# Attention and MoE in one kernel: ScalarE's exponentials ahead of the copies, weight pieces loaded four ahead, buffers moved

## The chip, the cores and the metric

The kernel runs on one core of a Trainium2 chip. The metric is device microseconds of one execution, the median of several runs. The engines are named as in the profile: PE is TensorE (PEld its weight loads), DVE is VectorE, ACT is ScalarE, POOL is GpSimd, SP is SyncE, whose queue issues nearly all DMAs.

## What is computed

Attention with rotary embedding over q, k, v of 4 x 8 heads x 576 x 64, then a feed-forward block with a convolution of three taps and a gate:

```python
q_rot, k_rot = (rotate(q), rotate(k))
scores = scale * np.matmul(q_rot, k_rot.transpose(0, 1, 3, 2))
scores = scores - np.max(scores, axis=-1, keepdims=True)
attn = np.exp(scores)
attn = attn / (np.sum(attn, axis=-1, keepdims=True) + 1e-09)
x = np.matmul(attn, v)              # heads side by side: 4 x 576 x 512
h = np.maximum(x @ w_in, 0.0)       # 512 x 1024
conv_out[:, t] = sum(conv_w[k] * hp[:, t + k] for k in range(3))
out = (h / (1.0 + np.exp(-conv_out))) @ w_out
```

All is in 32-bit floats. The weights arrive as 64-bit floats and are turned into 32-bit ones on the chip, each as a high and a low part.

## The kernel before

**Pairs and steps.** Two heads form a pair; there are 16 pairs, and each is worked in five steps (s = 0 to 4) of 128 rows of queries, the fifth with the last 64 rows of both heads. Steps are numbered through, n = 5p + s, from 0 to 79. For each step PE writes the scores into PSUM (`emit_S`, L254), DVE takes the negated row maxima of both heads (L269), ACT the exponentials of both with the row sums (L273). PE then transposes the result in 64 x 64 blocks (`emit_T`, L314, transposes L321) into two PSUM tiles, and ACT copies these two tiles to the buffer `pt` in SBUF (`out`, L337, copies through `evac`, L199). The next step's transposes go into the same two tiles. `emit_E` (L383, matmuls L389) multiplies the transposed probabilities of the pair before with v; in front of the MoE its result and that of `emit_Trem` (L352) lie in spare columns of the scores' PSUM tile, so the maxima of a step also wait for them. POOL applies the rotary embedding (L190, L193) to q and k of the coming pairs, DVE transposes them (L234, L237).

**Weights.** There are 16 pieces of 128 x 512 (`conv_w_piece`, L605): ACT takes the absolute value (L563), DVE does four passes (L566, L572, L577, L582), ACT writes the high part (L632), POOL the low one (L629). The first 13 pieces (`WEARLY`) are spread over steps 0 to 24, each load being issued by the last DVE pass of the piece three before; the buffer of a loaded piece exists four times. The last three pieces are placed by the table `LATEW`, which gives step and rank of their five parts.

**Order.** Each engine's order is the order in which the program emits. `at(n, rank, fn)` puts a function into step n; within a step the lower rank comes first. For steps below `WIDE` = 26 the ranks are: transposes 0, maxima 0.2, exponentials 0.3, parts of weight pieces 0.4, transposes of q and k 0.45, the next scores 0.5, `emit_E` 4, loads 18 to 19.6. From step 26 on, PSUM is laid out anew, with a pool for the MoE, and the MoE's units (`emit_M1`, L418, and `m2_half`, L527) are put between the steps. There, at step 26, the buffers of the MoE are opened and POOL clears their border columns (L783, L784); ACT's scaling by the first tap (L440) reads these borders.

**The lines of the change.** `emit_T` emitted the two copies directly after the transposes (L345); the last piece's first part stood in step 31 (L686); the load was issued three pieces ahead (L620); the MoE's buffers `rr` shared the pool `gpool` with the large buffer `gm` (L777 to L781).

Of the kernel before, what the change touches and what calls it, by code (L numbers as in the profile page):

```python
# [7 lines left out]
F32 = mybir.dt.float32  # L8
# [12 lines left out]
def attention_moe_kernel(ctx, tc, q, k, v, w_in, conv_w, w_out, tab, tabx, out):  # L21
# [9 lines left out]
    XW = HS + 2  # L31
# [43 lines left out]
    late = {"tail": False, "u": 0}  # L75
# [13 lines left out]
    def t_tile():  # L89
        return psum["t"].tile([128, 512], F32, tag="t", name="tp")  # L90
# [223 lines left out]
    def emit_T(p, s, h=None):  # L314
        if not h:
            tps[p] = [t_tile() for _ in range(2)]
        ps = tps[p]

        def turn(k, x, r):
            i = slice(64 * r, 64 * r + 64)  # L320
            nc.tensor.transpose(ps[r][:, 64 * k:64 * k + 64], x[i], idf[i, i])  # L321

        if s == 4:
            st = strem[p % 2]
            for t in range(4):
                for r in range(2):
                    turn(t, st[:, 128 * t:128 * t + 128], r)
            for r in range(2):
                turn(4, st[:, 512 - 64 * r:640 - 64 * r], r)
            evac("A", pt[:, 0:9:2, 512:S], ps[0][:, 0:320].rearrange("p (k c) -> p k c", k=5))  # L330
            evac("A", pt[:, 1:8:2, 512:S], ps[1][:, 0:256].rearrange("p (k c) -> p k c", k=4))
            evac("A", pt[64:128, 8, 512:S], ps[1][64:128, 256:320])
        else:
            for t in range(4):
                for r in range(2):
                    turn(2 * t + h, ST[p, s][:, h, 64 * h + 128 * t:64 * h + 128 * t + 128], r)
            def out():  # L337
                for r in range(2):
                    c = 128 * s + 64 * r
                    evac("A", pt[:, 0:8, c:c + 64], ps[r].rearrange("p (k c) -> p k c", k=8))  # L340

            if h and "m" in psum:
                at(late["n"], 2.2 if UNITS.get(late["n"]) == 2 else 1.6, out)
            elif h:
                out()  # L345

    def emit_Trem(p, s):
        x = ST[p, s].rearrange("p h k -> p (h k)")[:, 512:640]
# [249 lines left out]
    def load_w(i):  # L598
        src, _, _, kk, c = WPIECES[i]
        pool, bufs = wpool(i)  # L600
        t = pool.tile([128, 512], I64, tag="w64", name="w64", bufs=bufs + 1)
        nc.sync.dma_start(out=t, in_=src[kk * 128:kk * 128 + 128, c:c + 512])
        stage[i] = t

    def conv_w_piece(i):  # L605
        _, dh, dl, kk, c = WPIECES[i]
        box = {}

        def first():
            box["s"] = to_f32(*wpool(i), stage.pop(i), 512)  # L610
            box["s"][0]()

        def part(k):
            return lambda: box["s"][k]()

        def last():
            pool, bufs = wpool(i)
            box["w"] = pool.tile([128, 512], F32, tag="wf", name="wf", bufs=bufs)
            box["s"][4](box["w"])
            if i + 3 < WEARLY:  # L620
                load_w(i + 3)
            elif WEARLY <= i < len(WPIECES) - 2:
                load_w(i + 2)
            hi, lo = dh[:, kk, c:c + 512], dl[:, kk, c:c + 512]

            def low():
                for o in range(0, 512, 128):
                    w = slice(o, o + 128)
                    nc.gpsimd.tensor_tensor(out=lo[:, w], in0=box["w"][:, w], in1=hi[:, w].bitcast(F32), op=ALU.subtract)  # L629

            def high():
                nc.scalar.activation(out=hi, in_=box["w"], func=AF.Copy)  # L632

            if i < WEARLY:
                defer(2, lambda: (high(), low()))
            else:
                at(late["n"] + 1, 0.12, lambda: (high(), low()))

        return [first, part(1), part(2), part(3), last]

    def load_cw():
        t = stage["cw"] = ws.tile([32, 128], I64, tag="cw64", name="cw64", bufs=1)
        nc.gpsimd.memset(t.bitcast(I32), 0)
        nc.sync.dma_start(out=t[0:24, :], in_=conv_w.rearrange("k (c p) -> (k c) p", p=128))
# [26 lines left out]
    WEARLY = len(wcv) - 3  # L671
    COST = (1, 1, 0, 0, 1)
    wsteps = [(1, wcv[0][0])]
    for i in range(WEARLY):
# [8 lines left out]
    LATEW = (  # L683
# [3 lines left out]
    )  # L687
    plan = {}
    onpe = (0, 0.2, 0.5, 1, 2, 2.4, 3, 4, 10)
# [2 lines left out]
    def at(n, rank, fn):  # L692
        plan.setdefault(n, []).append((rank, len(plan.get(n, [])), fn))

    def emit():
        with tc.manual_schedule(engines=engines):
# [14 lines left out]
            load_v(0)  # L711
            load_w(2)
            load_cw()
            for p in range(1, NP):
                n = STEPS * p
                early = n - 10 >= WIDE - 1
                for i, part in enumerate("qk"):
                    if p > 1:
                        at(max(n - 10, WIDE) if early else n - 9 + 2 * i, 19.6 if early else 19, lambda p=p, part=part: load(p, part))
                    at(n - 8 + i if early else max(n - 6 + i, 0) if p > 1 else 0, 18, lambda p=p, part=part: rope(p, part))  # L720
                    at(n - 5 + i * (n - 10 < WIDE) if early else max(n - 4 + 2 * i, 2), 0.45, lambda p=p, part=part: emit_TQ(p, part))
                at(n + 1, 19, lambda p=p: load_v(p))
            for p in range(NP):
                n = STEPS * p
# [36 lines left out]
            for n, k in UNITS.items():  # L761
                for i in range(k):
                    blk, f = divmod(late["u"], NF)
# [5 lines left out]
            n = -1  # L769
            while any(plan.values()):  # L770
                n += 1
                late["n"] = n
                if n == WIDE:
                    wctx.close()
                    ectx.close()
                    psum_pools(actx, s=2, t=2, m=2)
                    gpool = ctx.enter_context(tc.tile_pool(name="gpool", bufs=1))  # L777
                    late["pc"] = ctx.enter_context(tc.tile_pool(name="pc", bufs=4))
                    late["po"] = ctx.enter_context(tc.tile_pool(name="po", bufs=1))
                    late["g"] = [gpool.tile([128, 2, NF, RA], F32R, name="gm")]  # L780
                    late["rr"] = [gpool.tile([128, XW + 1], F32, name=f"rr{i}") for i in range(4)]  # L781
                    for t in late["rr"]:
                        nc.gpsimd.memset(t[:, 0:1], 0.0)  # L783
                        nc.gpsimd.memset(t[:, XW:XW + 1], 0.0)  # L784
                if n == WIDE + 12:
                    lctx.close()
                    late["g"].append(ctx.enter_context(tc.tile_pool(name="gb", bufs=1)).tile([128, 2, NF, RING - RA], F32R, name="gb"))
                while plan.get(n):
                    e = min(plan[n], key=lambda e: e[:2])
                    plan[n].remove(e)  # L790
                    e[2]()
                    if e[0] in onpe and e[0] != (0 if n >= WIDE else 0.2):
                        tick()
# [72 lines left out]
```

## Time and profile before

| what | value |
|---|---|
| median of 3 runs | 490.39 us (490.19 to 491.83) |
| the profiled execution | 493.55 us, its span 491.8 us |
| mean granted clock of TensorE | 0.975 |
| busy: PE, DVE, ACT, POOL | 457.9, 355.7, 332.5, 300.9 us |
| chain that ended last: PE, DVE, ACT, DMA | 71%, 12%, 5%, 4% of the span |

The span runs from the first to the last instruction of the profiled execution; the execution's own time lies 1.75 us above it. Times in the rows are microseconds from the span's start. The busy time of PE is an upper bound, since matmuls are pipelined and their ends are modelled. The granted clock is a share of 2.4 GHz; the lower level is 1.2 GHz, a share of 0.5.

### The profile page before, as it was taken

The numbers are of one execution on the slowest core, as the hardware profiler recorded it, in microseconds if no ns is written. First come the engines' busy times: TensorE is split into PE (matmuls) and PEld (weight loads), VectorE is DVE, ScalarE is ACT, GpSimd is POOL, SyncE is SP. The second block draws the span as 40 slices with busy tenths as digits, with TensorE's granted clock in tenths as the row PEclk, the third lists the DMA queues.
The fourth block names the chain that finished last, engine by engine and source line by source line (L and its number), as shares of the span: only waits on it lengthen the run. The fifth ranks groups of instructions, "written<-read, shape, count | busy, mean of one in ns | idle before, by whom it ended". The sixth has DMA issues, their size and how long they took to land.

```text
span 491.8 us, 12405 instructions
## 1 busy us (share of the span) xinstructions
PE 457.9 (93%) x4572; PEld 361.2 (73%) x4572; DVE 355.7 (72%) x636; ACT 332.5 (68%) x951; POOL 300.9 (61%) x495
## 2 busy tenths in 40 slices
PE   1869879797898999999999999999999999999997
PEld 1436546464676788887979787878797979899886
DVE  5589978958598987686868686877774756467921
ACT  2587968777697878686878686868596864145510
POOL 3599889888669958485766757584721313244510
PEclk9989988979899899999999999999999999999999
DMA  8983885965445234253625190707020200100011
GB/s 224 168 175 104 168 191 112 172 146 119 97 93 109 37 73 98 62 98 75 93 61 110 38 131 19 150 14 140 29 61 13 60 13 25 45 21 23 0 63 44
DMA packets 140559, 42.71 MB, mean 87 GB/s; under 512 B 132156, under 2 KB 135252, under 8 KB 140500
## 3 DMA queue, kind: packets, MB, share of 16 engines
q1 hardware_dynamic: 139156, 41.54, 39.9%
q8 instruction: 36, 0.59, 0.5%
q10 hardware_dynamic: 1344, 0.39, 0.4%
q14 instruction: 23, 0.19, 0.1%
HBM read 37.12 MB, written 4.79 MB: 85 GB/s over the span
## 4 chain that ended last, share of the span: by engine, by line
PE 71%; DVE 12%; ACT 5%; DMA 4%; SPq 4%; POOL 3%; issue 2%; DVEq 0%; POOLq 0%; ACTq 0%
PE pm L428 13%; PE sp L261 12%; PE pm L537 11%; PE mt L517 10%; PE pm L389 10%; PE mt L428 7%; PE tp L321 5%; DVE negm L269 4%; DMA rq<-q 2%; ACT st L273 2%; POOL rk L190 2%; DVE wt L577 1%; DMA rd<-rt 1%; PE sp L389 1%; DVE wt L572 1%
## 5 line engine op out<-in xcount | busy, mean ns | idle before, releaser
L269 DVE TENSOR_REDUCE negm<-sp 128x1 f32<-128x576 f32 x144 | 102.6, 749 | 45.6 <-PE sp L261 30.3
L273 ACT ACTIVATE st<-sp,negm 128x576 f32<-128x576 f32 x128 | 93.8, 742 | 27.6 <-DVE negm L269 26.7
L261 PE MATMUL sp<-kT,qT 64*128 64x288 f32 (+4 forms) x556 | 103.5, 476 | 5.2 <-DVE kT L237 2.4
L199 ACT ACTIVATE pt<-tp 128x512 f32<-128x512 f32 (+3 forms) x176 | 84.0, 529 | 5.3 <-PE tp L321 4.8
L446 DVE SCALAR_TENSOR_TENSOR c<-rr,cw,c 128x288 f32<-128x288 f32 x128 | 79.4, 620 | 4.4 <-ACT c L440 0.2
L464 POOL TENSOR_TENSOR gm<-c,gm 128x288 fp32r<-128x288 f32 (+4 forms) x72 | 45.4, 635 | 52.7 <-ACT gm L463 52.5
L428 PE MATMUL pm<-xT,winh 128*128 128x290 f32 x352 | 75.9, 310 | 0.0
L190 POOL TENSOR_TENSOR rq<-rq,tabt 128x192 f32<-128x192 f32 x90 | 59.7, 696 | 14.5 <-DMA rq<-q 14.5
L261 PEld LDWEIGHTS sp<-kT,qT 64*128 64x128 f32 (+1 forms) x556 | 48.2, 182 | 26.3 <-issue 9.1
L410 POOL TENSOR_TENSOR xT<-xn,xT 128x290 fp32r<-128x290 f32 x32 | 28.1, 878 | 60.0 <-ACT xT L406 59.9
L321 PEld LDWEIGHTS tp<-idf,st 64*128 64x128 f32 x1024 | 43.2, 142 | 24.2 <-ACT st L273 13.2
L428 PEld LDWEIGHTS pm<-xT,winh 128*128 128x128 f32 x352 | 57.2, 192 | 1.8
L190 POOL TENSOR_TENSOR rk<-rk,tabt 128x192 f32<-128x192 f32 x90 | 54.9, 642 | 4.2 <-DVE c L455 4.2
L321 PE MATMUL tp<-idf,st 64*128 64x64 f32 x1024 | 48.6, 230 | 9.5 <-ACT st L273 9.4
L428 PE MATMUL pm<-xT,winl 128*128 128x290 f32 x176 | 52.6, 299 | 0.0
L389 PE MATMUL pm<-pt,vm 128*64 128x290 f32 x368 | 49.8, 411 | 0.4 <-ACT pt L199 0.4
L537 PE MATMUL pm<-wouth,gm 64*128 64x256 f32 x512 | 49.3, 282 | 0.0
L455 DVE SCALAR_TENSOR_TENSOR c<-c,rr 128x288 f32<-128x288 f32 x64 | 37.6, 609 | 9.6 <-ACT c L452 9.6
L537 PEld LDWEIGHTS pm<-wouth,gm 64*128 64x128 f32 x512 | 43.0, 185 | 0.0
L444 DVE TENSOR_SCALAR c<-rr,cw 128x288 f32<-128x288 f32 x56 | 24.0, 428 | 21.1 <-ACT rr L436 19.7
L537 PE MATMUL pm<-woutl,gm 64*128 64x256 f32 x256 | 38.8, 277 | 0.0
L389 PEld LDWEIGHTS pm<-pt,vm 128*64 128x64 f32 x368 | 25.6, 136 | 17.6 <-ACT pt L199 1.1
(119 smaller groups left out, 911.7 us busy)
## 6 DMA issues: line engine op xcount, KB each, us to landing
rq<-q SPq DMA_DIRECT2D x30, 144.0 KB
rq<-q SPq DMA_DIRECT2D x60, 72.0 KB
rk<-k SPq DMA_DIRECT2D x30, 144.0 KB
rk<-k SPq DMA_DIRECT2D x60, 72.0 KB
w<-moe_w_in SPq DMA_DIRECT2D x8, 512.0 KB
vm<-v SPq DMA_DIRECT2D x32, 128.0 KB
w<-moe_w_out SPq DMA_DIRECT2D x8, 512.0 KB
rb<-rd SPq DMA_DIRECT2D x16, 144.0 KB
```

Source lines behind the costliest of these rows:

```text
L190: nc.gpsimd.tensor_tensor(out=y, in0=y, in1=tabt[:, a:a + 3], op=ALU.mult)
L199: nc.scalar.activation(out=out, in_=in_, func=AF.Copy, scale=1.0 if sc is None else sc)
L261: nc.tensor.matmul(out=out, lhsT=qt[64 * h:64 * h + 64, c], rhs=kt[64 * h:64 * h + 64, a:a + n], start=True, stop=True)
L269: reds.setdefault((p, s), []).append(lambda: nc.vector.tensor_reduce(out=nm, in_=sc, axis=AX.XY if len(sc.shape) == 3 else AX.X, op=ALU.ma ...
L273: lambda: nc.scalar.activation(out=dst, in_=sc, func=AF.Exp, bias=nm, scale=1.0, accum_out=sm)
L321: nc.tensor.transpose(ps[r][:, 64 * k:64 * k + 64], x[i], idf[i, i])
L389: nc.tensor.matmul(out=xp[64 * h:64 * h + 64, :], lhsT=vmain[p][:, h, i, :] if i < 4 else vrem[p % 2][:, h, :], rhs=pt[:, 2 * i + h if i < ...
L428: nc.tensor.matmul(out=ps[:, 0:XW], lhsT=w[:, kk, fs], rhs=xT[:, xs, e, :], start=(i == 0), stop=(i == n - 1))
L446: nc.vector.scalar_tensor_tensor(out=c, in0=r[:, j + e:j + e + HS], scalar=cw[:, 8 * e + f:8 * e + f + 1], in1=c, op0=ALU.mult, op1=ALU.add,)
L464: nc.gpsimd.tensor_tensor(out=lo, in0=c[:, o:o + n], in1=hi.bitcast(F32), op=ALU.subtract)
L517: nc.tensor.matmul(out=ops[tt][:, 0:width], lhsT=g_tile(tt, f, e), rhs=w[:, f, cols], start=(f == 0 and i == 0), stop=(f == NF - 1 and i = ...
L537: nc.tensor.matmul(out=ps[r][:, 0:256], lhsT=g_tile(tt, f, e)[rows], rhs=w[rows, f, cols], start=(f == 0 and i == 0), stop=(f == NF - 1 an ...
```

## The change

It does four things. Below step 26 the two copies of a step's transposes are put at rank 0.32 of the step that emits the transposes, behind that step's exponentials (0.3). One more weight piece is loaded at the start, and each later load up to piece 12 is issued by the piece four before. The absolute value of the last piece moves from step 31 to step 32. The buffers `rr` get a pool of their own, opened first, and `gm` is opened last. The copies of the fifth step (s = 4) of a pair are emitted elsewhere (L330 to L332) and stay where they were.

```diff
             if h and "m" in psum:
                 at(late["n"], 2.2 if UNITS.get(late["n"]) == 2 else 1.6, out)
             elif h:
-                out()
+                at(late["n"], 0.32, out)
...
-            if i + 3 < WEARLY:
-                load_w(i + 3)
+            if i + 4 < WEARLY:
+                load_w(i + 4)
             elif WEARLY <= i < len(WPIECES) - 2:
                 load_w(i + 2)
...
-        ((31, 5.5), (33, 2.6), (33, 2.6), (34, 2.6), (34, 2.6)),
+        ((32, 5.5), (33, 2.6), (33, 2.6), (34, 2.6), (34, 2.6)),
...
             load_w(2)
             load_cw()
+            load_w(3)
...
                     psum_pools(actx, s=2, t=2, m=2)
-                    gpool = ctx.enter_context(tc.tile_pool(name="gpool", bufs=1))
+                    rpool = ctx.enter_context(tc.tile_pool(name="rpool", bufs=1))
+                    late["rr"] = [rpool.tile([128, XW + 1], F32, name=f"rr{i}") for i in range(4)]
                     late["pc"] = ctx.enter_context(tc.tile_pool(name="pc", bufs=4))
                     late["po"] = ctx.enter_context(tc.tile_pool(name="po", bufs=1))
+                    gpool = ctx.enter_context(tc.tile_pool(name="gpool", bufs=1))
                     late["g"] = [gpool.tile([128, 2, NF, RA], F32R, name="gm")]
-                    late["rr"] = [gpool.tile([128, XW + 1], F32, name=f"rr{i}") for i in range(4)]
```

ACT in step 16 (the fourth pair; step 16 emits the transposes of the probabilities of step 15), before; `pt<-tp` are the copies of the transposes, `st<-sp,negm` the exponentials, `wt` and `winh` parts of weight pieces:

```order
L632 ACTIVATE winh<-wf 128x512 [waits DVE_49]
L199 ACTIVATE pt<-tp 128x8x64 [waits PE_49] x2
L273 ACTIVATE st,sums<-sp,negm 128x576 [waits DVE_49]
L273 ACTIVATE st,sums<-sp,negm 128x576
L399 ACTIVATE xn<-sp 128x145 [waits Pool_49]
L563 ACTIVATE wt<-w_915 128x512 [waits DMAHW1_49]
```

and with the change:

```order
L632 ACTIVATE winh<-wf 128x512 [waits DVE_49]
L273 ACTIVATE st,sums<-sp,negm 128x576 [waits DVE_49,PE_49]
L273 ACTIVATE st,sums<-sp,negm 128x576
L199 ACTIVATE pt<-tp 128x8x64 [waits PE_49] x2
L399 ACTIVATE xn<-sp 128x145 [waits Pool_49]
L563 ACTIVATE wt<-w_796 128x512 [waits DMAHW7_49]
```

The two copies now stand behind both exponentials, and behind their wait for DVE's maxima. One wait holds for both exponentials.

SP's queue at the place that issued a load at 75.11 us, before (`rk` is k, `rd` the round trip of the row sums; `w_1023` is piece 10):

```order
L150 DMA rk<-k 32x18x32 [waits DMAHW6_49]
L151 DMA rk<-k 32x18x32 [waits DMAHW7_49]
L602 DMA w_1023<-moe_w_out 128x512 [waits DMAHW0_49,Activation_49]
L371 DMA rd<-rt 9x32 [waits DMAHW1_49,DVE_49]
L371 DMA rd<-rt 9x32 [waits DMAHW2_49]
```

and with the change (`w_1025` is piece 11):

```order
L150 DMA rk<-k 32x18x32 [waits DMAHW7_49]
L151 DMA rk<-k 32x18x32 [waits DMAHW0_49]
L602 DMA w_1025<-moe_w_out 128x512 [waits DMAHW1_49,DVE_49,Activation_49]
L371 DMA rd<-rt 9x32 [waits DMAHW2_49,DVE_49]
L371 DMA rd<-rt 9x32 [waits DMAHW3_49]
```

The same place in the queue now loads the next piece, and the load waits for DVE too, since it takes the buffer that DVE's last pass of piece 7 reads.

## Rows read from the trace of the kernel before

**Rows 1.** Busy time by stretch: length, PE, PEld, DVE, ACT, POOL, clock, DMA share, GB/s
```profile
42.00:62.00 20.00, 17.99 (x205) 11.27 (x202) 19.58 (x32) 17.87 (x47) 17.93 (x30) 1.00 0.73 147
...
70.00:78.00 8.00, 7.34 (x34) 3.46 (x36) 6.36 (x13) 6.22 (x18) 6.97 (x12) 0.57 1.04 217
78.00:97.00 19.00, 17.40 (x210) 11.66 (x210) 18.28 (x31) 15.14 (x41) 17.28 (x28) 1.00 0.60 120
...
101.00:106.00 5.00, 5.00 (x45) 3.43 (x43) 1.14 (x2) 3.07 (x8) 5.00 (x10) 0.59 0.46 116
...
175.00:470.00 295.00, 294.84 (x3122) 250.50 (x3119) 212.70 (x400) 202.41 (x604) 156.98 (x258) 1.00 0.29 60
```

**Rows 2.** Waits of ACT up to 118 us: in total, times, longest
```profile
ACT st L273 <- DVE negm L269: 9.0, 7, 4.4
...
ACT pt L199 <- PE tp L321: 4.3, 8, 2.0
```

**Rows 3.** Timeline 78 to 88 us, start and us: a step in front of the MoE
```profile
79.28 0.72 PE L321 MATMUL tp<-idf,st 64*128 64x64 f32 x16
...
80.02 1.09 ACT L199 ACTIVATE pt<-tp 128x512 f32<-128x512 f32 x2 [0.19 <-PE tp L321]
80.07 1.38 DVE L269 TENSOR_REDUCE negm<-sp 128x1 f32<-128x576 f32 x2
...
81.48 0.74 ACT L273 ACTIVATE st<-sp,negm 128x576 f32<-128x576 f32 x1 [0.38 <-DVE negm L269]
...
82.22 0.73 ACT L273 ACTIVATE st<-sp,negm 128x576 f32<-128x576 f32 x1
82.75 0.80 PE L321 MATMUL tp<-idf,st 64*128 64x64 f32 x16
...
82.87 1.42 DVE L269 TENSOR_REDUCE negm<-sp 128x1 f32<-128x576 f32 x2 [0.40 <-PE sp L389]
...
86.66 1.41 DVE L269 TENSOR_REDUCE negm<-sp 128x1 f32<-128x576 f32 x2
```

**Rows 4.** Timeline 91 to 106 us: the late weight piece and what followed
```profile
91.37 0.44 SPq L602 DMA_DIRECT2D w<-moe_w_out  x1
...
94.39 1.41 DVE L269 TENSOR_REDUCE negm<-sp 128x1 f32<-128x576 f32 x2
...
95.76 0.69 ACT L563 ACTIVATE wt<-w 128x512 f32<-128x512 f32 x1 [2.63 <-DMA w<-moe_w_out]
...
98.84 1.42 PE L321 MATMUL tp<-idf,st 64*128 64x64 f32 x16 [2.73 <-ACT st L273]
...
100.04 2.02 PE L261 MATMUL sp<-kT,qT 64*128 64x512 f32 x4
...
102.93 2.20 PE L389 MATMUL sp<-pt,vm 128*64 128x145 f32 x16
```

**Rows 5.** Timeline of PE: the same scores and matmuls at full clock
```profile
79.82 1.08 PE L261 MATMUL sp<-kT,qT 64*128 64x512 f32 x4
...
81.37 1.21 PE L389 MATMUL sp<-pt,vm 128*64 128x145 f32 x16
```

**Rows 6.** Timeline 74 to 83 us: DVE's last pass of a piece, SP's next transfer
```profile
78.20 0.97 DVE L582 SCALAR_TENSOR_TENSOR wf<-w,wt 128x512 int32<-128x512 int32 x1
...
80.17 1.36 SPq L371 DMA_DIRECT2D rd<-rt  x4
```

**Rows 7.** Timeline 112 to 132 us: POOL and ACT at the first steps of the MoE
```profile
113.05 1.92 POOL L629 TENSOR_TENSOR woutl<-wf,wouth 128x128 fp32r<-128x128 f32 x4 [3.84 <-ACT wouth L632]
...
129.66 0.09 POOL L783 MEMSET rr<- 128x1 f32 x1
...
129.79 0.53 ACT L440 ACTIVATE c<-rr,cw 128x288 f32<-128x288 f32 x1 [4.00 <-POOL rr L783]
```

**Rows 8.** Timeline 154 to 158 us: the last weight piece in step 31
```profile
155.25 1.41 DVE L269 TENSOR_REDUCE negm<-sp 128x1 f32<-128x576 f32 x2
...
155.36 0.68 ACT L563 ACTIVATE wt<-w 128x512 f32<-128x512 f32 x1 [1.10 <-DMA rq<-q]
```

## The prediction

> **What bounds the kernel now.** I read the stretches by stage first. From 175 to 470 us TensorE is busy for 294.84 of 295 us at full clock [rows 1]: nothing on ScalarE can shorten that part, and what the change is worth is read in front of it. There no engine is full by itself: from 42 to 62 us DVE works 19.58 of 20 us, TensorE and ScalarE 18, GpSimd 17.93; from 78 to 97 us DVE 18.28 and TensorE 17.40 of 19 [rows 1]. Two stretches in between run TensorE at a granted clock of 0.57 and 0.59, near its lower level of 1.2 GHz [rows 1].
>
> The list of waits comes next: up to 118 us ScalarE waits 9.0 us for DVE's row maxima (4.4 of it at the start, where it has nothing else to do), and 4.3 us for TensorE's transposes before it can copy them [rows 2]. Then the timeline of one ordinary step. I call the 16 transposes of a step T and the two copies of their result C. T of the step begins at 79.28 and lasts 0.72. C begins at 80.02. DVE's maxima of the next step start at 80.07 and end at 81.45, the two exponentials start at 81.48 and end at 82.95, the next T starts at 82.75, as soon as TensorE is through [rows 3]. So C fills ScalarE's time while DVE is still looking for the maxima.
>
> Last, the one long stall: the weight piece issued at 91.37 us is wanted at 93.13 and there at 95.76. ScalarE stands for 2.63 us, TensorE then for 2.73, and when TensorE goes on, it goes at the low clock: 0.59 from 101 to 106 us [rows 1, 4].
>
> **The exponentials ahead of the copies** concern the four C of steps s = 0 to 3 in each of five head pairs, 20 in all; nothing is added. Two things bound what this gives. It gains only where ScalarE waits for T while the maxima are ready: at most the 4.3 us of [rows 2], of which 2.0 is one wait right behind the long stall. It loses where the maxima come after T. T writes the same two PSUM tiles as the T before, so it must wait until C is through. In the step of [rows 3] the exponentials can't start before 81.45, so C now runs from 82.95 to 84.04 (1.09, as at 80.02), and the next T starts at 84.0 in place of 82.75: 1.2 us lost on TensorE. The maxima that follow on DVE started at 86.66; TensorE would have given their scores 1.2 us later than now, DVE was then 0.3 us behind TensorE, so about 0.9 of the 1.2 passes through. Walking the rest of this pair the same way (each T at the later of TensorE's turn and the end of C) the pair ends 1.0 us later: a second step costs nothing new, since exponentials and T are then late together. Of the five pairs I take four at this price, 1.0 us each; in the second DVE is full without a break (the row from 42 to 62 us of [rows 1]), T comes later and nobody waits for it. Sum +4.0, bounds 0 (DVE hides all of it) and 5 x 1.2 = +6.0.
>
> **Pieces four ahead.** The load that stood at 91.37 us is now issued at the place of the load before it, some 15 us earlier, and the stall of [rows 4] goes. What it cost: TensorE's wait of 2.73 less the 0.5 that remains (maxima end at 95.80, the first exponential 0.74 later, TensorE is ready at 96.1), so 2.2; and the low clock behind it. There the sixteen matmuls at 102.93 took 2.20 and the scores at 100.04 took 2.02, at full clock 1.21 and 1.08 [rows 4, 5]; with T 1.42 for 0.72 [rows 3, 4] that is 0.99 + 0.94 + 0.70, and about 0.55 for the three small groups in the same proportion: 3.2. Gain 5.4 us; bounds 2.2 (the clock falls anyway) and 5.9. What is late next is GpSimd, below. The new wait: each load now takes the buffer of a piece that DVE must have finished. At the tightest place DVE is done at 79.17 and the next transfer in SP's queue starts at 80.17 because it waits for DVE anyway [rows 6]: cost 0. The fourth piece joins the opening loads; it stands behind the first q and k in the queue, so 0, at most +1.0 if it delays the next q by two such transfers.
>
> **Buffers moved.** The first Relu of the MoE loses its wait for GpSimd and ScalarE. It did not stand on that wait: the scaling after it is what stood, 4.00 us, for the border memsets, and those stay behind the rope on GpSimd's queue [rows 7]. Worth 0.
>
> **Third late piece a step later.** Its Abs stood 1.1 us on ScalarE at 155.36. The row names a DMA, but it also reuses a buffer whose last reader on DVE stands right ahead of the maxima that start at 155.25, and that is the later one. The exponentials behind it need maxima that start at 155.25 and end at 156.66 [rows 8]; they started at 156.79. Worth 0.1.
>
> **The sum.** Entering the MoE: -5.4 + 4.0 = -1.4 us. There the memsets bind: GpSimd runs without a break from 113.05 to 129.7, released at 113.05 by ScalarE after a wait of 3.84 [rows 7]. That release is a copy of a weight piece behind the maxima of its step; it comes earlier by 1.4, less the C (about 0.7 net) that now stands in front of it: -0.7. So the end moves by -0.7 - 0.1 = **-0.8 us**. The profiled execution took 493.55 us (span 491.8, 1.75 around it), 3.16 above the median of the three runs, 490.39. I take the difference over: **489.6 us**, no change that can be told, since about 0.3% (1.5 us) is what a measurement of this kernel can tell.
>
> **Rivals.** (1) The delay is swallowed: the maxima wait for DVE nearly everywhere, as from 42 to 62 us, and the 20 later C cost nothing. Then ScalarE arrives 5.4 us earlier, and the gate is GpSimd alone, whose wait of 3.84 us goes whole: -3.8 - 0.1, **486.5 us**. For it: DVE at 18.28 and 19.58 in two stretches [rows 1]. Against: at 82.87 DVE itself waited 0.40 for TensorE [rows 3], so there it has no cover.
>
> (2) The gaps bring the clock down, slower. The swap makes TensorE stand 1.1 to 1.2 us at one step of nearly every pair, and longer in the first pair, where there is no other work between scores and T. One fall of the clock costs the 3.2 us worked out above; the point that decides is whether a gap of this size is enough. After 2.73 us it fell [rows 4]; from 78 to 97 us, with waits that left TensorE 17.40 of 19 busy, it stayed at 1.00 [rows 1]. With one fall on the path and the swap's upper bound: -0.8 + 3.2 + 2.0 = +4.4 at the most, +2.4 with the swap as priced: **492.8 us**, up to 494.8. The Trainium skill, "TensorE: Matmul & The Clock Gate", section "A second HAM failure mode: psum-queue depth-cycling", says that short, frequent idles between groups of matmuls can make the clock go back and forth between its levels, without a long gap. By that rule this rival would be the likely one, at two falls or +5.6; this trace does not bear it out in the ordinary steps, where short waits left the clock at 1.00 [rows 1].
>
> (3) It doesn't do what it says: the early piece is on time, but the place is bound by GpSimd's rope and its loads, which the change leaves alone, so that the gate at 129.79 [rows 7] stands where it stood: 490.3 us, inside the forecast.
>
> **How the numbers follow.** The forecast with its own range (swap +2 to +6, stall -5.4 or -2.2 at the worst; -2.5 to +1.5 us) has 0.45, with (3) in it; rival 1 has 0.28; rival 2 has 0.27. Faster by over 0.3%: nearly all of rival 1 and a third of the forecast's range, 0.42. Within 0.3%: the rest of the forecast's range but for a little, and the near ends of both rivals, 0.31. Slower by over 0.3%: most of rival 2 and a little of the forecast's range, 0.27. The range that holds 8 in 10 goes from 485.5 (rival 1 with a us more) to 494.0 (most of rival 2); the likeliest case alone 487.9 to 491.9.
>
> **What would show it.** Right: no wait of ScalarE for a piece of moe_w_out near 95 us and a clock of 1.00 in that pair; DVE's total of waits on TensorE's scores up, ScalarE's waits on maxima up from 9.0; T some 1.0 to 1.2 us after the scores in front of it, in the first, third, fourth and fifth pair; the copies behind the exponentials never waiting for T; the memset at 129.0 +- 0.7. Wrong: pairs that take as long as before (swap costs nothing, the memset near 126); a low clock in a pair that had full clock, or a low stretch that is longer (rival 2); the opening rope waiting for q near 33 us, which would be the price of the fourth piece.

## The result, and the profile after

| | median | range | runs |
|---|---|---|---|
| before | 491.24 us | 490.19 to 491.83 | 6 |
| with the change | 494.6 us | 492.77 to 496.13 | 6 |

The ratio is 1.0068, 95% interval 1.0048 to 1.0088: **slower by 3.3 us**. The forecast was 489.6 us, its range ended at 494.0. Executions over 1.5% above the fastest of their kernel are left out of every ratio.

The two profiled executions don't stand at the same place of their runs: that of before took 493.55 us and is slower than all six shown, that of the change took 492.77 and is the fastest of its six. TensorE's mean granted clock differs from one execution to the next, too: 0.976 to 0.990 in the change's six. So the traces differ by -0.8 us where the medians differ by +3.4. I compare stages, and name the low stretches where they decide.

The change, busy time by stretch, as in [rows 1], with four stretches more:

```profile
42.00:62.00 20.00, 17.23 (x193) 10.98 (x193) 17.93 (x29) 18.01 (x50) 15.90 (x27) 1.00 0.76 143
70.00:78.00 8.00, 5.00 (x29) 2.74 (x31) 5.38 (x12) 6.46 (x17) 3.81 (x9) 0.67 0.83 168
78.00:97.00 19.00, 18.07 (x187) 11.65 (x186) 16.90 (x29) 15.21 (x41) 16.82 (x26) 0.87 0.47 106
97.00:106.00 9.00, 8.55 (x100) 5.71 (x101) 8.54 (x15) 8.30 (x24) 9.00 (x15) 1.00 0.69 125
106.00:117.00 11.00, 8.85 (x95) 5.38 (x93) 9.32 (x17) 8.24 (x22) 11.00 (x19) 1.00 0.70 158
117.00:125.00 8.00, 7.08 (x38) 3.81 (x40) 4.11 (x8) 5.74 (x16) 8.00 (x14) 0.57 0.50 116
130.00:137.00 7.00, 6.61 (x72) 5.54 (x71) 5.26 (x8) 5.73 (x17) 4.28 (x16) 1.00 0.34 59
175.00:470.00 295.00, 294.84 (x3123) 249.67 (x3120) 213.98 (x400) 202.21 (x604) 158.08 (x258) 1.00 0.30 60
```

The kernel before, the same view, the four stretches that [rows 1] doesn't have:

```profile
97.00:106.00 9.00, 7.13 (x61) 4.86 (x63) 4.97 (x9) 6.72 (x18) 9.00 (x16) 0.62 0.57 135
106.00:117.00 11.00, 9.14 (x109) 5.73 (x105) 9.51 (x18) 8.76 (x24) 7.16 (x14) 1.00 0.64 138
117.00:125.00 8.00, 6.97 (x60) 4.80 (x62) 6.04 (x12) 6.51 (x18) 8.00 (x14) 1.00 0.51 121
130.00:137.00 7.00, 6.21 (x46) 5.13 (x47) 3.91 (x8) 5.79 (x17) 3.20 (x6) 0.76 0.36 59
```

The steady part from 175 us on is untouched. At 97 to 106 us, behind the late piece, the clock rose from 0.62 to 1.00, as forecast. But a stretch that had 1.00, 117 to 125 us, now has 0.57, and the low stretch near 75 us reaches further (78 to 97 us: 0.87 instead of 1.00). And GpSimd (the fifth pair of numbers) works 9.00 of 9, 11.00 of 11 and 8.00 of 8 us: from 97 us to the MoE it doesn't stand at all, where before it worked 7.16 of the middle 11. The low stretches of before at 130 to 137 us (0.76) and 157 to 163 us (0.73) are missing in the execution with the change (1.00 in both); they lie behind the entry into the MoE, and there this trace gains what lets it end earlier.

The change, waits up to 118 us, as in [rows 2] (the second list is that of SP's queue):

```profile
ACT st L273 <- DVE negm L269: 15.5, 13, 4.4
PE tp L321 <- ACT pt L199: 14.6, 24, 3.1
...
ACT pt L199 <- PE tp L321: 1.3, 2, 1.1
...
PE tp L321 <- ACT st L273: 0.8, 3, 0.3
...
SPq L602 <- DVE wf L582: 9.9, 4, 5.2
```

The waits turned round. ScalarE's wait for T fell from 4.3 to 1.3 us, its wait for maxima rose from 9.0 to 15.5, and TensorE's wait for copies, absent before, stands at 14.6 us in 24 places. Not all of that is lost. Before, T waited for the exponentials in the same places:

```profile
PE tp L321 <- ACT st L273: 9.4, 13, 2.7
...
PE tp L321 <- ACT str L273: 3.4, 4, 1.5
```

`str` is the fifth step's exponentials. These 12.8 us are down to 0.8, so that T's waits grew from 12.8 to 15.4 us in all, though the 2.73 us of the stall are gone from them. SP stands 9.9 us for DVE's last pass of a piece before it can issue the next load; before, no such wait is listed. There, too, a part is a change of place: SP's wait for the row sums (L371) fell from 8.2 to 2.6 us.

The change, the step that answers to [rows 3]:

```profile
83.30 0.72 PE L321 MATMUL tp<-idf,st 64*128 64x64 f32 x16
83.44 1.42 DVE L269 TENSOR_REDUCE negm<-sp 128x1 f32<-128x576 f32 x2 [0.34 <-PE sp L389]
...
84.96 0.74 ACT L273 ACTIVATE st<-sp,negm 128x576 f32<-128x576 f32 x1 [2.17 <-DVE negm L269]
...
86.41 1.08 ACT L199 ACTIVATE pt<-tp 128x512 f32<-128x512 f32 x2
86.89 1.42 DVE L269 TENSOR_REDUCE negm<-sp 128x1 f32<-128x576 f32 x2 [0.93 <-PE sp L389]
...
87.06 0.27 PE L321 MATMUL tp<-idf,st 64*128 64x64 f32 x1 [0.21 <-ACT pt L199]
...
87.54 0.71 PE L321 MATMUL tp<-idf,st 64*128 64x64 f32 x15 [0.22 <-ACT pt L199]
```

ScalarE stands 2.17 us with the finished T in front of it, then takes the exponentials, then copies. The next T starts 3.76 us after this one (3.47 before), waits once for each of the two copies, and DVE's next maxima wait 0.93 us for TensorE, 0.40 before. The scores behind this T start 4.20 us after the scores before them (83.84 and 88.04), against 3.57 before: the step costs TensorE 0.6 us, half of the 1.2 that the prediction walked through at this place.

The change, GpSimd and ScalarE on the way into the MoE, as in [rows 7]:

```profile
97.12 4.20 POOL L190 TENSOR_TENSOR rq<-rq,tabt 128x192 f32<-128x192 f32 x6
...
131.14 0.10 POOL L785 MEMSET rr<- 128x1 f32 x1
...
131.27 0.54 ACT L440 ACTIVATE c<-rr,cw 128x288 f32<-128x288 f32 x1 [2.36 <-POOL rr L785]
```

The same rope of q in the timeline of the kernel before:

```profile
93.43 3.85 POOL L190 TENSOR_TENSOR rq<-rq,tabt 128x192 f32<-128x192 f32 x6 [1.48 <-DMA rq<-q]
```

The chain that ended last runs over GpSimd here, in both traces. Where GpSimd begins its unbroken run, the change is late: the rope of q starts at 97.12 instead of 93.43, +3.7 us. GpSimd's wait of 3.84 us at the late piece is gone, and its work took 34.0 us instead of 32.4 (131.14 - 97.12, and 129.66 - 93.43 - 3.84). Sum: +3.7 - 3.84 + 1.6 = +1.5 us at the memsets, 131.14 against 129.66.

But TensorE is nearly as late. The change, TensorE from the fifth step of the fifth pair to the entry:

```profile
117.37 1.28 PE L321 MATMUL tp<-idf,str 64*128 64x64 f32 x10 [1.48 <-ACT pt L199]
119.08 4.13 PE L389 MATMUL tp<-pt,vm 128*64 128x290 f32 x16 [0.43 <-ACT pt L199]
...
132.27 0.39 PE L358 MATMUL pm<-idf,st 64*128 64x64 f32 x2 [0.39 <-ACT pt L199]
```

and before:

```profile
116.46 0.52 PE L321 MATMUL tp<-idf,str 64*128 64x64 f32 x10 [1.47 <-ACT str L273]
117.51 2.17 PE L389 MATMUL tp<-pt,vm 128*64 128x290 f32 x16 [0.52 <-ACT pt L199]
...
130.79 0.38 PE L358 MATMUL pm<-idf,st 64*128 64x64 f32 x2 [1.57 <-ACT pt L199]
```

L358 waits for a copy of ScalarE's that stands behind the scaling in its order, and the scaling waits for the memsets. TensorE stood 1.57 us for that copy before and 0.39 with the change, so its own work brought it there at 129.22 and 131.88: +2.7 us, more than GpSimd's +1.5. Of this 0.9 was there at the fifth step's T; the rest came behind it, where the low stretch lies and the sixteen matmuls took 4.13 us instead of 2.17.

### The profile page after: what moved, and what is told of

Same layout as the page of the kernel before. It is cut to its first block, busy times and chain, and to the rows that moved or that the text cites. A ratio compares the mean times of both kernels' runs of the same rounds, so it can differ in the third digit from the quotient of the medians.

```text
span 491.0 us, 12385 instructions
## 1 busy us (share of the span) xinstructions
PE 457.6 (93%) x4572; PEld 358.6 (73%) x4572; DVE 357.4 (73%) x636; ACT 332.4 (68%) x951; POOL 304.1 (62%) x495
## 4 chain that ended last, share of the span: by engine, by line
PE 73%; DVE 6%; POOL 5%; ACT 5%; DMA 4%; SPq 4%; issue 2%; DVEq 0%; ACTq 0%; POOLq 0%
PE pm L428 14%; PE sp L261 12%; PE pm L389 11%; PE pm L537 11%; PE mt L517 10%; PE mt L428 7%; PE tp L321 6%; ACT st L273 2%; DVE negm L269 2%; DMA rk<-k 2%; ACT pt L199 2%; POOL woutl L629 2%; SPq L150 2%; PE sp L389 2%; POOL rk L190 1%
## 5 line engine op out<-in xcount | busy, mean ns | idle before, releaser
L261 PE MATMUL sp<-kT,qT 64*128 64x288 f32 (+4 forms) x556 | 101.5, 468 | 2.6 <-ACT st L273 1.5
L428 PE MATMUL pm<-xT,winh 128*128 128x290 f32 x352 | 74.6, 306 | 0.0
L190 POOL TENSOR_TENSOR rq<-rq,tabt 128x192 f32<-128x192 f32 x90 | 60.7, 709 | 12.2 <-DMA rq<-q 12.2
L261 PEld LDWEIGHTS sp<-kT,qT 64*128 64x128 f32 (+1 forms) x556 | 47.2, 179 | 24.6 <-issue 9.7
L428 PEld LDWEIGHTS pm<-xT,winh 128*128 128x128 f32 x352 | 56.2, 189 | 1.8
L455 DVE SCALAR_TENSOR_TENSOR c<-c,rr 128x288 f32<-128x288 f32 x64 | 39.7, 641 | 9.6 <-ACT c L452 9.6
L537 PEld LDWEIGHTS pm<-wouth,gm 64*128 64x128 f32 x512 | 41.8, 185 | 0.0
L537 PE MATMUL pm<-woutl,gm 64*128 64x256 f32 x256 | 37.6, 276 | 0.0
```

Source lines behind the costliest of these rows:

```text
L190: nc.gpsimd.tensor_tensor(out=y, in0=y, in1=tabt[:, a:a + 3], op=ALU.mult)
L261: nc.tensor.matmul(out=out, lhsT=qt[64 * h:64 * h + 64, c], rhs=kt[64 * h:64 * h + 64, a:a + n], start=True, stop=True)
L428: nc.tensor.matmul(out=ps[:, 0:XW], lhsT=w[:, kk, fs], rhs=xT[:, xs, e, :], start=(i == 0), stop=(i == n - 1))
L537: nc.tensor.matmul(out=ps[r][:, 0:256], lhsT=g_tile(tt, f, e)[rows], rhs=w[rows, f, cols], start=(f == 0 and i == 0), stop=(f == NF - 1 an ...
```

## The experiments

Each was timed beside the kernel before on the same chip; ratios are to it, with their 95% intervals. The microseconds behind a ratio are worked out from it with 491.

**1. The parts one by one.** `a_noswap` is the change with the copies back in front:

```diff
-                at(late["n"], 0.32, out)
+                out()
```

> The change without its first part: the copies stand in front of the exponentials again, the loads four ahead, the later last piece and the buffers stay. Theory M (the reordering costs more than it was priced at, the early load gains as priced): the end is then set by GpSimd's gate alone, whose wait of 3.84 us goes, so about -3.8 us against the kernel before, with the border memset near 126 us. Theory R (the reordering is free and the loads crowd the opening): slower than before by the same 3.4 us as the whole change. In both the late piece near 95 us is on time.

Measured 0.9983 (0.9963 to 1.0003): -0.8 us. `b_swap` is the kernel before with that one line changed the other way.

> The kernel before with the exponentials ahead of the copies, and nothing else. Theory M: slower by 4 to 7 us, since each pair in front of the MoE loses 1 us or more to transposes that wait for copies, part of it hidden by the stall at the late piece that stays; TensorE's waits for copies about 15 us as in the whole change. Theory R: within 1 us of the kernel before.

Measured 1.0088 (1.0055 to 1.0121): **+4.3 us**. TensorE's waits for copies are 14.3 us, as expected. But the stall at the late piece, which was expected to stay, is gone, though the load is issued as late as before. `b_swap`, the load, ScalarE's first part of the piece and TensorE's fifth step of the fourth pair:

```profile
95.24 0.44 SPq L602 DMA_DIRECT2D w<-moe_w_out  x1
...
99.38 0.82 PE L321 MATMUL tp<-idf,str 64*128 64x64 f32 x10
...
99.77 0.76 ACT L563 ACTIVATE wt<-w 128x512 f32<-128x512 f32 x1
```

and its stretch behind the piece:

```profile
97.00:106.00 9.00, 8.50 (x90) 5.17 (x91) 8.51 (x15) 8.37 (x24) 8.00 (x12) 1.00 0.90 173
```

ScalarE comes so late to the piece that it has landed, and the clock behind it is 1.00. From the fifth step's T of the fourth pair to that of the fifth TensorE takes 19.93 us (99.38 to 119.31), as in the change (97.33 to 117.37, 20.04); before, with the stall, it took 23.63 (92.83 to 116.46).

`c_four` is the kernel before with the loads:

```diff
-            if i + 3 < WEARLY:
-                load_w(i + 3)
+            if i + 4 < WEARLY:
+                load_w(i + 4)
...
+            load_w(3)
```

> The kernel before with loads four ahead (and the fourth piece at the start), nothing else. Theory M: -3.8 us as in the run without the reordering, since the other two parts are worth nothing. Theory R: +3.4 us. If the three first runs do not add up, the parts work on each other.

Measured 1.0034 (0.9995 to 1.0073), +1.7 us. `d_bufs` has the pools' order and the later last piece.

> The kernel before with the buffers moved and the last piece's first part in step 32, nothing else. Both theories: within 1 us of the kernel before. More than 1 us either way would put a part of the result here, as neither expects.

Measured 1.0011 (0.9981 to 1.0041). So the whole loss is the reordering's; the early loads, forecast at -5.4 on TensorE and expected at -3.8, are worth nothing that can be told by themselves. The three parts alone add up to +6.5 us against +3.3 together, each with an interval of 1.5 to 1.9 us either way; whether they work on each other at the end, these times don't settle. Theory M is half wrong: where did the gain go? With the reordering the rows of `b_swap` answer: there is no stall left to save. Without it the question stays.

**2. The loads in two halves, the gate, one pair.** `e_late` loads three ahead up to piece 10 and only makes the late piece early, `k_early` does the opposite half.

```diff
-            if i + 3 < WEARLY:
+            if i + 3 < WEARLY and i <= 7:
                 load_w(i + 3)
-            elif WEARLY <= i < len(WPIECES) - 2:
+            if i + 4 < WEARLY and i >= 7:
+                load_w(i + 4)
+            if WEARLY <= i < len(WPIECES) - 2:
```

> The kernel before, three pieces ahead up to piece 10; the last pass of piece 7 loads pieces 10 and 11, and from there on it is four ahead. The opening keeps its loads, only the late piece is early. Theory M2 (the gain of the early piece is capped by GpSimd, which runs without a break from some 97 us to the memsets but for the one wait of 2.0 to 3.8 us that the late piece makes; loads four ahead in the opening hold up SP's queue and cost 1 to 2 us): GpSimd's wait near 112 us goes, the opening is as before, 2 to 3.8 us faster than before and 1 to 2 us faster than the run with all loads four ahead. Rival (the early piece only moves the wait or the low clock elsewhere): within 1 us of before.

> The other half: loads four ahead from the start up to piece 10, the late piece 11 as late as before. Theory M2: SP waits some 5 us in all for DVE's last passes before it can issue the pieces' loads, what stands behind them in its queue (round trip of the row sums, q, k) comes later, 1 to 2 us slower than before, and the stall at the late piece stays. Rival: within 1 us of before.

Measured 0.9976 (0.9947 to 1.0005) and 1.0029 (0.9998 to 1.0060): -1.2 and +1.4 us. Neither alone is clear of no change. They point the way M2 said, but `e_late` falls short of its 2 to 3.8 us, and the rival, within 1 us, isn't excluded for either. `k_early`, SP's waits up to 75 us:

```profile
SPq L602 <- DVE wf L582: 7.0, 4, 2.7
SPq L374 <- DMA rd<-rt: 5.3, 2, 2.9
```

and `d_bufs`, three ahead, in the same stretch (it has no wait of the first kind):

```profile
SPq L374 <- DMA rd<-rt: 3.4, 2, 2.3
```

The load waits 7.0 us in all at the head of SP's queue, the round trip of the row sums lands later behind it, and q with it: GpSimd's rope of q at 52 to 54 us waited 2.20 us for it in `k_early`, 1.65 in `d_bufs`, and 3.14 in `a_noswap`. Most of the 7.0 us takes the place of other waits at the head of the queue (for q's transposes 1.6 instead of 4.2, for the row sums 0.5 instead of 2.7), and the rope of q started at 53.00 in `k_early`, 53.96 in `a_noswap`, 52.36 in `d_bufs`, 52.77 before: 0.2 to 1.6 us later.

`f_border` lets DVE clear the border columns (`nc.vector.memset` for `nc.gpsimd.memset`).

> The kernel before with the eight clearings of border columns on DVE in place of GpSimd, nothing else: the gate measured by itself. If GpSimd's memsets alone hold the entry into the MoE, ScalarE's wait of 4.0 us goes and the kernel is 2 to 4 us faster. If the rope of k, which ends only 0.1 us in front of the memsets, is wanted at the same place, 0 to 1 us.

Measured 0.9988 (0.9963 to 1.0013), -0.6 us, the second branch: clearing the borders earlier doesn't bring the entry forward. ScalarE's scaling does start 3.8 us earlier there and waits for nothing, but the next exponentials stand at 129.26, behind maxima that wait for TensorE:

```profile
125.99 0.54 ACT L440 ACTIVATE c<-rr,cw 128x288 f32<-128x288 f32 x1
```

`h_swap1` and `g_swap0` reorder one pair alone:

```diff
+            elif h and p == 1:
+                at(late["n"], 0.32, out)
             elif h:
                 out()
```

> The kernel before with the exponentials ahead of the copies in the second pair alone (steps 6 to 9), which the prediction priced at 0 since DVE is full there. Theory M2: the pair itself becomes 1.5 to 2.4 us longer (from the first transposes of step 6 to those of step 11), and this passes to the end through GpSimd, 1 to 2 us slower. The prediction's price: within 0.5 us.

> The kernel before with the exponentials ahead of the copies in the first pair alone (steps 1 to 4), priced at 1.0 us in the prediction. If the price of the whole reordering (+4.3 us) is spread over the pairs: 0.5 to 1.5 us slower. If gaps in the first pair bring the clock down (there is no other work between scores and transposes): a low stretch near 26 to 33 us and 2 us or more.

Measured 1.0037 (1.0012 to 1.0063) for the second pair, +1.8 us, and 0.9992 (0.9965 to 1.0019) for the first. `g_swap0` has the low stretch that its second branch spoke of (granted clock 0.50 from 28 to 31 us). What that cost isn't shown: the trace of before has a low stretch of its own in this pair, 0.65 from 34 to 38 us, where `g_swap0` has 1.00. `h_swap1` in the second pair, ScalarE, then TensorE:

```profile
42.31 1.08 ACT L199 ACTIVATE pt<-tp 128x512 f32<-128x512 f32 x2
...
42.96 0.27 PE L321 MATMUL tp<-idf,st 64*128 64x64 f32 x1 [2.38 <-ACT pt L199]
```

and the stretch behind it (length, PE busy, clock, DMA share, GB/s):

```profile
43.00:48.00 5.00, 4.78 (x37) 0.66 0.31 86
```

The same stretch of `d_bufs`, which has no reordering:

```profile
43.00:48.00 5.00, 5.00 (x70) 1.00 0.47 124
```

Here is rival 2 in one pair: the copies behind the exponentials make TensorE stand 2.38 us, and it goes on at 0.66. In the execution of the whole change the same T waited 2.22 us and the clock stayed at 1.00 (38 to 62 us), so a gap of about this size doesn't always bring it down.

**3. Is it GpSimd? A test that failed.** GpSimd's low parts of pieces 11 and 12 (L629, 1.7 to 1.9 us each) aren't needed in front of the MoE. Four kernels put them at the end of step 27: `l_low` on `d_bufs`, `m_after_low` on the change, `q_late_low` on `e_late` with the buffers, `n_best` that one with the border columns on DVE.

```diff
-            if i < WEARLY:
+            if i in (11, 12):
+                defer(2, high)
+                at(WIDE + 1, 19.9, low)
+            elif i < WEARLY:
                 defer(2, lambda: (high(), low()))
```

> The kernel before with the buffers' order of the change, and with GpSimd's low parts of weight pieces 11 and 12 put behind the entry into the MoE (emitted at the end of step 27); loads and copies as before. Theory G (GpSimd, without a break from some 97 us, sets the entry into the MoE): its work in front of the memsets shrinks by 3.4 to 3.8 us, and its wait for piece 11's high part goes too; ScalarE's wait of 4.0 us at the scaling goes, 3 to 4 us faster than before. Rival N (TensorE's and DVE's own chain is as late as GpSimd): within 1 us.

> The whole change plus the same move of GpSimd's two low parts. Theory G: the delay that the reordering and the opening's loads made no longer passes through GpSimd; ScalarE's wait of 2.36 us goes, 2 to 2.5 us faster than the whole change (494.6), still 0 to 2 us slower than before. Rival N: as slow as the whole change, +3.4 us.

> Copies in front of the exponentials, three ahead up to piece 10 and the late piece 11 early, the buffers of the change, GpSimd's two low parts behind the entry. Theory G: with GpSimd relieved, the gain of the early piece on TensorE (4 to 5 us at the late piece) is no longer capped, so 4 to 6 us faster than before and 1 us or more faster than the run with the low parts alone. Rival N: as that run.

> The run before this one with the border columns cleared by DVE. Theory G: GpSimd is no longer last at the entry, so this is worth 0 to 1 us; if the memsets are still what ScalarE waits for, 1 to 2 us.

Measured 1.0071 (1.0052 to 1.0091), 1.0149 (1.0112 to 1.0187), 1.0058 (1.0030 to 1.0087) and 1.0080 (1.0047 to 1.0112): all slower, the first two beyond either theory. From the memsets to the end the traces of the first three take 365.0 to 366.2 us; the twelve traces with the memsets on GpSimd and without this move take 359.5 to 362.1. So the loss lies behind the memsets. `l_low`, timeline of GpSimd and ScalarE:

```profile
137.83 5.19 POOL L629 TENSOR_TENSOR woutl<-wf,wouth 128x128 fp32r<-128x128 f32 x12
141.18 0.44 ACT L463 ACTIVATE gm<-c 128x288 fp32r<-128x288 f32 x1 [4.97 <-POOL woutl L629]
```

Three low parts now stood in one block in front of the rope of k, and ScalarE's first write of `gm` stood 4.97 us for them. The memsets did come early in `l_low` (126.85; 135.74 in `m_after_low`), but the place was wrong, and the runs say nothing of the theory.

**4. The same move, put where GpSimd is idle.** `r_low2` on `d_bufs` and `s_after_low2` on the change emit the two low parts at `at(WIDE, 0.01, low)`, directly behind the memsets, where GpSimd waited 3.8 us for q anyway. `j_late_border` is `e_late` with the buffers and the border columns on DVE, `t_best2` that one with the two low parts.

> As the run with GpSimd's two low parts moved, but they stand directly behind the memsets, where GpSimd waits 3.8 us for q, instead of in front of the rope of k. Theory G (GpSimd's unbroken run sets the entry): the memsets come 2 to 3 us earlier and nothing behind them is later, 1.5 to 3.5 us faster than before. Rival N (TensorE and DVE are as late there as GpSimd): within 1 us of before.

> The whole change with the same move. Theory G: 2 to 2.5 us faster than the whole change, so 1 to 2 us slower than before. Rival N (the reordering's delay stands on TensorE and DVE as well as on GpSimd): +3.4 us as the whole change.

> No reordering; the late piece alone early, buffers of the change, border columns on DVE, the two low parts behind the entry. Theory G: the early piece is no longer capped, 3 to 6 us faster than before. Rival N: 1 to 2 us faster, as the early piece and the border columns alone.

> The run before this one without the move of the low parts. Theory G: GpSimd caps it, 1 to 2 us faster than before. Rival N: as fast as the run with the move.

Measured: `r_low2` 0.9973 (0.9956 to 0.9991), -1.3 us; `s_after_low2` 1.0023 (1.0001 to 1.0046), +1.1 us; `j_late_border` 0.9962 (0.9933 to 0.9990), -1.9; `t_best2` 0.9942 (0.9922 to 0.9962), -2.8. With GpSimd relieved the whole change goes from +3.3 to +1.1 us, intervals apart, as theory G said. Without the reordering the move gives 1.3, a little less than expected. The traces say that GpSimd isn't alone. `r_low2`, then `s_after_low2`:

```profile
112.97 0.80 POOL L410 TENSOR_TENSOR xT<-xn,xT 128x290 fp32r<-128x290 f32 x1 [4.40 <-ACT xT L406]
```

```profile
115.83 0.80 POOL L410 TENSOR_TENSOR xT<-xn,xT 128x290 fp32r<-128x290 f32 x1 [1.09 <-ACT xT L406]
...
124.03 0.80 POOL L410 TENSOR_TENSOR xT<-xn,xT 128x290 fp32r<-128x290 f32 x1 [1.17 <-ACT xT L406]
```

Relieved of the low parts, GpSimd waits for ScalarE instead. Against the kernel without the move the memsets come 0.2 us earlier in `r_low2` (127.24, 127.47 in `d_bufs`) and 1.0 in `s_after_low2` (130.11, 131.14 in the change); for `r_low2` theory G expected 2 to 3. These are one execution each. Whether the move adds to the early piece (`t_best2` against `j_late_border`) their intervals leave open.

**5. The wait that took the stall's place.** In `t_best2`, with no stall at the late piece, GpSimd, DVE and TensorE at the next pair:

```profile
106.61 1.86 POOL L193 TENSOR_TENSOR rk<-rk 128x192 f32<-128x192 f32 x3
...
108.50 0.78 DVE L237 STREAM_TRANSPOSE kT<-rk 128x576 f32<-128x576 f32 x1 [1.57 <-POOL rk L193]
109.43 1.13 PE L261 MATMUL sp<-kT,qT 64*128 64x512 f32 x4 [2.15 <-DVE kT L237]
...
112.67 0.79 PE L321 MATMUL tp<-idf,str 64*128 64x64 f32 x10 [1.58 <-ACT str L273]
```

GpSimd ends the rope of k, DVE transposes it, TensorE waits 2.15 us for it, and from 113 to 122 us it runs at a granted clock of 0.67, near the lower of its two levels. `u_low9` puts the low part of piece 9 behind this rope as well (`at(20, 18.5, low)`).

> The fastest version so far (no reordering, late piece early, border columns on DVE, the low parts of pieces 11 and 12 behind the entry) with one step more: the low part of piece 9 stands behind the rope of k on GpSimd instead of in front of it. Theory G: the wait that takes the stall's place, TensorE's for the transposed k (2.15 us at 109.43, released by GpSimd's rope through DVE), shrinks by GpSimd's 1.7 us to about 0.5 us; 1.5 us faster than that version if the low clock behind it stays, 3 to 5 us if that goes too. Rival N: the wait stays or moves, within 0.5 us.

Measured 0.9919 (0.9893 to 0.9944), **-4.0 us**. Its row in TensorE's timeline at that place:

```profile
109.01 1.13 PE L261 MATMUL sp<-kT,qT 64*128 64x512 f32 x4 [0.45 <-DVE kT L237]
```

The wait fell from 2.15 to 0.45 us, by GpSimd's 1.7; the low clock stayed (0.66 from 113 to 122 us). The intervals of `u_low9` and `t_best2` touch, so the step's own 1.2 us isn't settled, but this version beats both kernels clearly. It has the early piece, the buffers' order, DVE's border columns and GpSimd's three low parts out of the way, and not the reordering; which of these it needs was not taken apart.

In most profiles the low stretch moves when the stall goes, but not in all. The granted clocks at 97 to 106 us, then at 113 to 122 us: with the stall `d_bufs`, `l_low` and `r_low2` have 0.81, then 1.00, but `k_early`, stalled for 4.00 us, 0.62 and 0.82, `g_swap0` 0.81 and 0.81, `h_swap1` 0.81 and 0.86, and `f_border`, whose ScalarE waited 1.65 us for the piece, 1.00 and 0.62. Without the stall `a_noswap`, `c_four`, `j_late_border`, `t_best2` and `u_low9` have 1.00, then 0.81, 0.74, 0.71, 0.67, 0.66, and so have the change (0.72), `b_swap` (0.87), `q_late_low` (0.62) and `n_best` (0.67), but `s_after_low2` and `m_after_low` have 1.00 in both. `s_after_low2`, the later stretch (length, PE busy, clock, DMA share, GB/s):

```profile
113.00:122.00 9.00, 6.58 (x61) 1.00 0.84 196
```

## Why the prediction was wrong

**The reordering: the sum right by luck, the places wrong.** Forecast +4.0 in front of the MoE, measured alone +4.3 (2.7 to 5.9). The mechanism is the one that was walked through: T waits for copies that stand behind maxima and exponentials. But the first pair, priced at 1.0, cost nothing (-1.7 to +0.9), and the second, priced at 0 because DVE was full there, cost +1.8 (0.6 to 3.1). A busy share of 19.58 in 20 us [rows 1] didn't mean that nobody waited: in `h_swap1` DVE itself stood 2.54 us for TensorE in that pair. (The row, 42 to 62 us, also holds only the later half of that pair, whose fifth step's T starts at 52.33.) And the total fits because two misses cancel. In `b_swap` TensorE reaches the fifth step's T of the fourth pair 6.6 us later than before (99.38 and 92.83), where the forecast has 3.0 up to there; in the fifth pair it gets 3.7 back, because the stall has gone. These are one execution each.

**Pieces four ahead: the step that failed.** The sum "-5.4 + 4.0" sets the whole price of the stall against the reordering, as if the stall stood there whatever the reordering does. It doesn't: with the reordering alone the late load is in time, the clock behind it is 1.00, and the fifth pair takes 19.93 us on TensorE, with the early load 20.04. So the early load had next to nothing left to gain: the change is 1.0 us ahead of `b_swap`, within the noise. Without the reordering the stall does go by the early load (in `a_noswap` the fifth pair takes 20.22 us, against 23.63 before and 22.43 in `d_bufs`), which is 2.2 to 3.4 us on TensorE and not 5.4; at the end it is -0.8 us (-1.8 to +0.1) in `a_noswap`, -1.2 (-2.6 to +0.2) in `e_late`. What takes the rest back is shown in part only:

- "The new wait: cost 0" was read at one place. In the opening, loads four ahead stand in SP's queue for DVE's last pass, and q comes later; `k_early` measures +1.4 us (-0.1 to +2.9), not clear of nothing.
- The 3.2 us of low clock weren't saved in most of the profiled executions. Without the stall TensorE reaches the next pair before GpSimd's rope is ready, waits there (1.33 us in `a_noswap`, 2.15 in `t_best2`) and then for the exponentials, and a low stretch comes at 113 us instead of 98. That the wait is GpSimd's is shown by `u_low9`; that it brings the clock down is not, since the low stretch outlived it. In the change itself this wait is 0.47 us, and the two waits in front of its low stretch (1.48 and 0.43) are as long as before (1.47 and 0.52), where the clock stayed at 1.00. What brings this low stretch stays open.
- What is left may be capped by GpSimd's own wait, 3.84 us [rows 7] in that execution, 2.02 in `d_bufs`. This is argued: `t_best2` against `j_late_border` doesn't settle it.

**The way from there into the MoE: the wrong sign.** The prediction let gain and loss meet on TensorE (-5.4 + 4.0), and only then asked GpSimd ("-0.7"). But GpSimd's run begins at 93 us, ahead of the stall and behind nearly four reordered pairs. So in this execution GpSimd took the delay in full, +3.7, and of the gain no more than its own wait, 3.84; its work became 1.6 us longer. Forecast for the memsets 129.0 +- 0.7, measured 131.14. That GpSimd has a part in it is shown by `s_after_low2`: 2.2 us of the loss go when it has two low parts less to do. That it is the only path is not: in the change's execution TensorE comes to the entry 2.7 us later than before by its own work, and the relieved GpSimd soon waits for ScalarE.

**The range.** It ended at +1.5 us, though the bounds of its own terms (reordering +6.0, stall -2.2) reach +3.8 on TensorE alone; the result, +3.3, lies within them.

**Buffers and last piece.** Forecast 0 and -0.1, together measured +0.5 (-0.9 to +2.0).

**The rivals.** Rival 1 (delay swallowed) and rival 3 are out. Rival 2's price, 492.8 to 494.8, holds the result, and its signs are there: low stretches after gaps that the reordering made (`h_swap1` at 43 us, the first pair in `g_swap0`). But it doesn't explain the whole. The low stretch at 117 us comes without the reordering too (`a_noswap`). And there is hardly more low clock in all: the mean granted clock of the change's six executions has the median 0.979, that of `b_swap` 0.979, that of before, timed beside `b_swap`, 0.982. A mean lower by 0.003 is, by estimate, 1.5 us of work at full clock in 491, and costs as much only if all of it is on the path. The one execution of the change at 0.990 took 494.53 us, about the median. The Trainium skill, "TensorE: Matmul & The Clock Gate", section "A second HAM failure mode: psum-queue depth-cycling", says that short, frequent idles between groups of matmuls can make the clock go back and forth, and so speaks for this rival. Here the runs agree in part: in `u_low9` the clock fell behind waits of 0.45, 1.61 and 0.53 us, none long, while the change kept 1.00 from 38 to 62 us through a wait of 2.22 us and shorter ones.

**Open:** the medians put the change 3.3 us behind, its fastest execution puts the memsets only 1.5 us later. From the memsets to the end the spans took 359.9 us (change) and 360.0 (`d_bufs`), but 362.1 in the profiled execution of before, whose clock was low at 130 to 137 us and at 157 to 163. What a median execution of the change looks like was not recorded.

## What to carry to other kernels

Before a stall's cost is put down as a gain beside a loss ahead of it, ask whether that loss alone lets the late transfer arrive in time: then the stall is gone without its cure, and the two don't add. Then look for the engine that is late next at that place, and from where on it works without a break: a delay ahead of that point reaches it, and a gain behind it is worth at most that engine's own wait. A buffer that is loaded one piece earlier without one more copy of it can turn a free load into a wait at the head of the queue; load early the piece that is late. Putting a producer's work ahead of the copies that free its input tiles costs wherever that work's own inputs come later than the tiles, and a full engine next to it is no cover.

## What was not expected of the hardware

- The granted clock didn't follow the length of a single gap: it stayed at 1.00 after a wait of 2.22 us in the change's second pair, and fell to 0.66 after 2.38 us at the same place in `h_swap1`.
- The same GpSimd work between the rope of q and the memsets, its waits taken off, took 32.3 us in `d_bufs` (127.47 - 93.11 - 2.02), 32.4 before, 32.9 in `c_four` and 33.3 in `a_noswap`, but 34.0 in the change and 34.1 in `b_swap`, the two with the reordering; the four low operations of one piece alone took 1.69 us at the shortest and 2.97 at the longest. What stretches them was not tried.
